# Fewer, larger transfers in a decode block: V's last two tiles in one, wo in 32 and 16 parts

## The chip, the cores and the metric

The kernel runs on one core of a Trainium2 chip. A core has TensorE (PE, matrix multiply), VectorE (DVE), ScalarE (ACT), GpSimd (POOL) and SyncE (SP), which here issues every DMA, and sixteen DMA engines that move the data from HBM (the chip's main memory) to SBUF (the core's working memory). Matmuls write to PSUM, in banks. The metric is the device time of one execution in microseconds (us), as the median of several runs; the profile describes one further execution.

## What is computed

One block of a transformer in decoding: two sequences of one token each, D = 640, 32 heads of 192, a window of the last 1024 positions of a cache of 4096, and a feed-forward part with F = 1536. All inputs are bfloat16.

```python
mod = (silu(c) @ w_mod).reshape(2, 6, 1, -1)
sa, ca, ga, sb, cb, gb = (mod[:, i] for i in range(6))
h = layernorm(x) * (1 + ca) + sa
q = (h @ wq).reshape(B, 1, 32, 192).transpose(0, 2, 1, 3)
k = k_cache[:, :, 3072:, :]; v = v_cache[:, :, 3072:, :]
p = softmax(einsum('bhqd,bhkd->bhqk', q, k) * 192 ** -0.5)
o = einsum('bhqk,bhkd->bhqd', p, v)
x = x + ga * (o.transpose(0, 2, 1, 3).reshape(B, 1, 6144) @ wo)
h = layernorm(x) * (1 + cb) + sb
x = x + gb * ((gelu(h @ w_gate) * (h @ w_up)) @ w_down)
```

K and V of the window are 25.2 MB each (32 heads, 1024 positions, 192 numbers of 2 bytes, two sequences), the largest share of the 76.88 MB that are read.

## The kernel before

**Memory.** `ring` has four slots of 24,576 bytes per partition, and `r1` takes the place of more: first it holds wq, then two tiles ("slots" 4 and 5), then wo. A tile of K or V is a quarter of one sequence's window: 128 partitions stand for 32 heads times four stretches of 256 positions, and a tile holds 64 of these positions for each. There are 16 tiles, eight of K and eight of V. The list `items` (line 336) says how they are loaded: kind, sequence, first tile, number of tiles, slot, semaphore. All entries take two tiles at once except the last two, which are tiles 2 and 3 of V of sequence 1, into slots 2 and 3. The semaphore counts 16 for each finished transfer (one for each DMA engine).

**The order of the transfers.** SyncE issues the transfers in the order of the program, and each issue waits for the instructions that last used the place that it overwrites. In order: w_mod, c, x, wq, the four K transfers, the V transfers, wo, w_gate, w_up, w_down in parts of 6, 4 and 2 of its twelve. `load_kv(n)` (line 344) issues `items` up to the n-th. The calls stand in the program where the place has just come free: the V transfers of sequence 1, tiles 2 and 3, come behind `weighted(0, 0, 2)`, because they overwrite tiles 0 and 1 of V of sequence 0 (slots 2 and 3). wo goes to `r1`, and its transfers wait for the last two PV steps of sequence 0 (line 603 on). w_gate, w_up and w_down go to slots 0 and 1 and wait for the first two PV steps of sequence 1 (`r3_dead`, line 607).

**The order of the work.** After the modulation, the first layer norm and q come the scores: DVE multiplies a half tile of K by q (line 465), PE sums with an identity matrix (line 476), DVE reduces (line 483). Then both softmaxes. Then PV: for each tile DVE spreads the weights over a mask (`d_mask`, line 511, two buffers in turn) and PE multiplies by the tile (`p_pv`, line 523, 32 matmuls of 384 columns). After the last tile of sequence 1 come `p_sel(0)` (line 548), `normalize(1)` (four small steps, ACT and DVE in turn, lines 536 and 540) and `p_sel(1)`. The result is copied out (lines 432 and 434) and turned by three DVE transposes of 16 parts each (line 597, `OT_SPLIT`).

**wo.** The 6144 rows of wo are 48 parts of 128 rows, a partition holding one row of each part. The parts are loaded and multiplied in groups, `WO_SPLIT`. A group's matmuls (line 628, four for each part, each on 32 columns of the array) wait for the group's transfer and for the transposes of its parts. The groups are multiplied in order.

**Fillers.** `warm(n, bank)` (line 454) puts n matmuls into PE's order whose result nobody reads; they keep PE busy. `WO_WARM` says how many follow each group of wo. Twelve follow the statistics of the second layer norm, eight follow w_gate, five w_up and five the first part of w_down.

**Behind wo.** Line 634 multiplies by ga, `layer_norm("ln2", ...)` ends with hT, w_gate's matmuls (line 646) feed the gelu on ACT (line 653), w_up's matmuls (line 646) the product on DVE (line 660) and its transpose, and w_down's three parts (line 669) follow. Two vector steps (lines 676 and 678) and the store of the output end the program.

Of the kernel before, what the change touches and what calls it, by code (L numbers as in the profile page):

```python
# [103 lines left out]
def bass_adaLN_cond__sliding_block_cached__geglu_ffn__decode_kernel(  # L104
# [49 lines left out]
    NS = 4  # L154
    SL = J * Dh
    WQ_SPLIT = [5]
    assert sum(WQ_SPLIT) == KT
    WO_SPLIT = [16, 16, 12, 4]
    OT_SPLIT = [16, 16, 16]
    assert sum(WO_SPLIT) == NT and sum(OT_SPLIT) == NT  # L160
    WU_SPLIT = [5]
# [2 lines left out]
    assert sum(WD_SPLIT) == FT  # L164
    ND = 4

    WO_WARM = [0, 8, 0, 9]
    WU_WARM = [5]
    WD_WARM = [5, 0, 0]

# [1 line left out]
    with es:  # L172
        S = _Sched(nc, es)
# [21 lines left out]
        def tile_f(slot, n=1):  # L195
            if slot < NS:
                return ring_f[:, slot * SL:(slot + n) * SL]
            return r1[:, (slot - NS) * SL:(slot - NS + n) * SL]
# [60 lines left out]
        def bank(k):  # L259
            return ("bank", k)  # L260
# [4 lines left out]
        sem_wq = [S.sem("d_wq%d" % i) for i in range(len(WQ_SPLIT))]  # L265
        sem_wo = [S.sem("d_wo%d" % i) for i in range(len(WO_SPLIT))]
        sem_wg = S.sem("d_wg")
        sem_wu = [S.sem("d_wu%d" % i) for i in range(len(WU_SPLIT))]
        sem_wd = [S.sem("d_wd%d" % i) for i in range(len(WD_SPLIT))]
        sem_ring = [S.sem("d_ring%d" % i) for i in range(4)]  # L270
        sem_out = S.sem("d_out")

        def k_dma(dst, src):
            return lambda e: e.dma_start(dst, src)  # L274
# [48 lines left out]
        def ring_keys(slot):  # L323
            return [half_key(slot, 0), half_key(slot, 1)]
# [9 lines left out]


        items = [("k", 0, 0, 2, 0, 0), ("k", 0, 2, 2, 2, 1), ("k", 1, 0, 2, NS, 2), ("k", 1, 2, 2, 0, 0), ("v", 0, 0, 2, 2, 1),
                 ("v", 0, 2, 2, NS, 2), ("v", 1, 0, 2, 0, 0), ("v", 1, 2, 1, 2, 1), ("v", 1, 3, 1, 3, 3)]
        place = {(kind, b, t0 + i): slot + i for kind, b, t0, nt, slot, _ in items for i in range(nt)}
        assert NTL == 4 and len(place) == 4 * NTL

# [3 lines left out]
        def load_kv(upto, deps=()):  # L344
            while keep["kv"] < upto:
                kind, b, t0, nt, slot, sm = items[keep["kv"]]
                cache = A_v_cache if kind == "v" else A_k_cache
                S.dma("sp", k_dma(tile_f(slot, nt),
                                  cache[b, :, K0:Sk, :].rearrange("h (q r) d -> h q r d", q=QP)[:, :, J * t0:J * (t0 + nt), :].rearrange("h q r d -> h q (r d)")),
                      sem_ring[sm], writes=[k for i in range(nt) for k in ring_keys(slot + i)], deps=deps, name="ld_%s%d_%d" % (kind, b, t0))  # L350
                keep["kv"] += 1
# [98 lines left out]
        def warm(n, bk):  # L450
            def f(e):
                last = None
                for _ in range(n):
                    last = e.matmul(ps[:, bk, 0:2 * Dh], lhsT=ident_b[:, :], rhs=qbc[:, :, :].rearrange("p b d -> p (b d)"),  # L454
                                    start=True, stop=True)
                return last
            if n:
                S.op("pe", f, reads=["ident_b", "qbc"], writes=[bank(bk)], name="warm")
# [104 lines left out]
        def weighted(b, ta, tb):  # L563
            for t in range(ta, tb):
                d_mask(b, t)
                p_pv(b, t)
# [10 lines left out]
        softmax(0)  # L577
        softmax(1)
        weighted(0, 0, 2)
        load_kv(9)  # L580
        weighted(0, 2, 4)
        normalize(0)
        for t in range(NTL):
# [17 lines left out]
        wo_src = A_wo.rearrange("(p t) n -> p t n", t=NT)  # L601
        wo_of = [(sum(WO_SPLIT[:i]), sum(WO_SPLIT[:i + 1])) for i in range(len(WO_SPLIT))]
        for i, (ta, tb) in enumerate(wo_of):
# [19 lines left out]
        for i, (ta, tb) in enumerate(wo_of):  # L623
# [7 lines left out]
            S.op("pe", f, reads=[("wo", i)] + [("oT", t) for t in range(ta, tb)], writes=[bank(BK_M)], name="wo%d" % i)  # L631
            warm(WO_WARM[i], 1)

# [82 lines left out]
```

## Time and profile before

| what | value |
|---|---|
| median of 3 runs | 187.02 us (186.99 to 187.12) |
| the profiled execution | 187.01 us |
| its span, first to last instruction | 185.7 us |
| PE, DVE, ACT, POOL busy | 117.2, 106.6, 13.9, 4.9 us |
| read from HBM | 76.88 MB, 414 GB/s over the span |
| mean granted clock of PE | 0.915 |

How to read what follows. Times count in microseconds from the first instruction. PEld is the loading of weights into PE, which overlaps the matmuls. The digits of a busy row are tenths in 40 equal slices of the span. A timeline's line gives the start, the length, the engine, the line of the program, the operation with its tiles and shapes, the count, and in brackets the idle time before it and what ended that. "DMA ring<-in_B_w_down_dram" is the stretch from a transfer's issue to its landing. A transfer is cut into packets, here one for each partition, and it has landed when all sixteen engines have written their last; beside the views, the trace records each packet's size and duration, the landing on each engine, and the times at which the granted clock changed. SPq is SyncE's queue of instructions.

### The profile page before, as it was taken

How to read it: one execution, taken by the hardware profiler on the slowest of the kernel's cores; microseconds unless marked ns; L12 is line 12 of the kernel's file. 1: busy time of each engine (PE TensorE's matmuls, PEld its weight loads, DVE VectorE, ACT ScalarE, POOL GpSimd, SP SyncE). 2: the span in 40 equal slices, each digit the busy share in tenths (PEclk: the TensorE clock that was granted, in tenths of full speed). 3: DMA queues.
4: the chain of work that ended last, by engine and by line, in shares of the span. 5: the costliest groups of instructions: out<-in, count | busy, mean ns of one | idle time of the engine just before them, and what ended most of it. 6: DMA issues, size and time to landing. Idle time of an engine off the chain costs nothing.

```text
span 185.7 us, 2254 instructions
## 1 busy us (share of the span) xinstructions
PE 117.2 (63%) x1014; PEld 60.8 (33%) x1014; DVE 106.6 (57%) x114; ACT 13.9 (7%) x24; POOL 4.9 (3%) x12
## 2 busy tenths in 40 slices
PE   0004500871079899988999885349928977299844
PEld 0001200440024334433344342226614654265422
DVE  6801600020598999999999993294556714803331
ACT  2001400013000000000000000200010004100400
POOL 8200000000000000000000000000000000000000
PEclk9999999998559999999999999558996999859999
DMA  7999998898999989899999989899999999999991
GB/s 248 414 437 477 463 463 389 371 491 371 487 413 434 468 381 459 381 487 402 455 424 434 459 381 466 381 487 413 395 434 424 424 435 424 413 408 435 422 392 50
DMA packets 2925, 77.02 MB, mean 415 GB/s; under 512 B 356, under 2 KB 356, under 8 KB 868
## 3 DMA queue, kind: packets, MB, share of 16 engines
q1 hardware_dynamic: 2916, 76.88, 96.7%
q8 instruction: 8, 0.13, 0.3%
q14 instruction: 1, 0.01, 0.0%
HBM read 76.88 MB, written 0.00 MB: 414 GB/s over the span
## 4 chain that ended last, share of the span: by engine, by line
DMA 43%; DVE 36%; PE 16%; SPq 1%; ACT 1%; issue 1%; POOL 1%; DVEq 0%; POOLq 0%
DMA ring<-in_A_k_cache_dram 24%; DVE ring L465 19%; DMA ring<-in_B_w_down_dram 18%; PE ps L523 10%; DVE r L465 7%; DVE Sg L483 5%; PE ps L476 4%; DVE Em L511 2%; SPq L274 1%; ACT E_sb L502 1%; PE ps L504 1%; PE ps L498 1%; DVE On L540 0%; ACT On L536 0%; PE ps L491 0%
## 5 line engine op out<-in xcount | busy, mean ns | idle before, releaser
L465 DVE TENSOR_TENSOR ring<-ring,qbc 128x6144 bf16<-128x6144 bf16 x12 | 40.1, 3351 | 8.4 <-DMA ring<-in_A_k_cache_dram 8.4
L476 PE MATMUL ps<-ring,ident_b 128*128 128x512 bf16 x144 | 34.7, 393 | 13.0 <-DVE ring L465 13.0
L454 PE MATMUL ps<-qbc,ident_b 128*128 128x384 bf16 x120 | 24.7, 339 | 0.7 <-ACT qbc L432 0.7
L523 PE MATMUL ps<-ring,Em 128*64 128x384 bf16 x192 | 19.6, 371 | 7.8 <-DVE Em L511 6.6
L476 PEld LDWEIGHTS ps<-ring,ident_b 128*128 128x128 bf16 x144 | 13.6, 100 | 32.7 <-DVE ring L465 17.2
L511 DVE TENSOR_TENSOR Em<-E_sb,M32b 128x2048 bf16<-128x2048 bf16 x8 | 18.1, 2288 | 5.5 <-PE ps L523 5.5
L523 PEld LDWEIGHTS ps<-ring,Em 128*64 128x64 bf16 x192 | 12.4, 125 | 14.6 <-DVE Em L511 7.3
L454 PEld LDWEIGHTS ps<-qbc,ident_b 128*128 128x128 bf16 x120 | 11.6, 101 | 10.9 <-issue 2.8
L401 PE MATMUL ps<-ring,scT 128*32 128x480 bf16 x40 | 4.4, 601 | 16.0 <-DVE scT L358 16.0
L465 DVE TENSOR_TENSOR r<-r,qbc 128x6144 bf16<-128x6144 bf16 x4 | 13.4, 3352 | 0.0
L483 DVE TENSOR_REDUCE Sg<-ps 128x32 f32<-128x512 f32 x16 | 11.0, 687 | 3.4 <-PE ps L476 3.4
L424 PE MATMUL ps<-r,hT 128*32 128x384 bf16 x80 | 5.8, 475 | 10.7 <-DMA r<-in_A_wq_dram 10.7
L476 PE MATMUL ps<-r,ident_b 128*128 128x512 bf16 x48 | 11.1, 380 | 1.8 <-DVE r L465 1.8
L434 DVE CAST aux<-ps 128x384 bf16<-128x384 f32 x4 | 2.0, 553 | 16.6 <-PE ps L424 15.7
L628 PE MATMUL ps<-r,aux 128*32 128x160 bf16 x192 | 5.1, 271 | 4.4 <-DMA r<-in_A_wo_dram 2.6
L424 PEld LDWEIGHTS ps<-r,hT 128*32 128x32 bf16 x80 | 3.2, 135 | 13.8 <-issue 11.6
L476 PEld LDWEIGHTS ps<-r,ident_b 128*128 128x128 bf16 x48 | 4.4, 98 | 8.1 <-DVE r L465 3.4
L401 PEld LDWEIGHTS ps<-ring,scT 128*32 128x32 bf16 x40 | 1.2, 132 | 17.5 <-DVE scT L358 16.0
L540 DVE TENSOR_SCALAR On<-ps,rden 32x192 bf16<-32x192 f32 x4 | 1.7, 418 | 8.9 <-ACT On L536 8.9
L502 ACT ACTIVATE E_sb<-Sg,nb 128x256 bf16<-128x256 f32 x2 | 1.0, 507 | 75.6 <-DVE nb L501 75.6
L628 PEld LDWEIGHTS ps<-r,aux 128*32 128x32 bf16 x192 | 4.3, 114 | 5.8 <-DMA r<-in_A_wo_dram 3.6
L523 PE MATMUL ps<-r,Em 128*64 128x384 bf16 x64 | 5.4, 327 | 0.0
(73 smaller groups left out, 65.6 us busy)
## 6 DMA issues: line engine op xcount, KB each, us to landing
ring<-in_A_k_cache_dram SPq DMA_DIRECT2D x3, 6144.0 KB, 40.3
ring<-in_A_v_cache_dram SPq DMA_DIRECT2D x2, 6144.0 KB, 23.3
r<-in_A_wq_dram SPq DMA_DIRECT2D x1, 7680.0 KB, 30.7
r<-in_A_k_cache_dram SPq DMA_DIRECT2D x1, 6144.0 KB, 38.4
r<-in_A_v_cache_dram SPq DMA_DIRECT2D x1, 6144.0 KB, 23.3
ring<-in_A_v_cache_dram SPq DMA_DIRECT2D x2, 3072.0 KB, 17.6
r<-in_A_wo_dram SPq DMA_DIRECT2D x2, 2560.0 KB, 23.7
ring<-in_w_mod_dram SPq DMA_DIRECT2D x1, 4800.0 KB, 14.2
```

Source lines behind the costliest of these rows:

```text
L274: return lambda e: e.dma_start(dst, src)
L401: last = e.matmul(ps[SQ * j:SQ * j + SQ, bk, 0:3 * DN].rearrange("p (i n) -> p i n", i=3), lhsT=scT[:, k, :], rhs=wm_v[:, k, 3 * part * D: ...
L424: last = e.matmul(ps[SQ * j:SQ * j + SQ, BK_H + c, 0:QC], lhsT=hT[:, k, :], rhs=wq_v[:, k, RN * j + QC * c:RN * j + QC * (c + 1)], start=( ...
L434: S.op("dve", lambda e: e.tensor_copy(out=dst, in_=src), reads=reads, writes=writes, name=name)
L454: last = e.matmul(ps[:, bk, 0:2 * Dh], lhsT=ident_b[:, :], rhs=qbc[:, :, :].rearrange("p b d -> p (b d)"), start=True, stop=True)
L465: S.op("dve", lambda e: e.tensor_tensor(out=tile_v(ks)[:, hf * JH:(hf + 1) * JH, :], in0=tile_v(ks)[:, hf * JH:(hf + 1) * JH, :], in1=qbc[ ...
L476: last = e.matmul(o_ap, lhsT=ident_b[:, :], rhs=tile_v(ks)[:, hf * JH:(hf + 1) * JH, ci * GC:(ci + 1) * GC], start=(ci == 0), stop=(ci == ...
L483: S.op("dve", lambda e: e.tensor_reduce(out=S_sb[:, b, a:a + JH], in_=ps[:, hf, 0:JH * GC].rearrange("p (j c) -> p j c", j=JH), axis=AX.X, ...
L502: S.op("act", lambda e: e.activation(out=E_sb[:, b, :], in_=S_sb[:, b, :], func=ACTF.Exp, scale=SCALE, bias=nb[:, 0:1], accum_out=esum[:, ...
L511: S.op("dve", lambda e: e.tensor_tensor(out=Em[:, t % 2, :, :], in0=E_sb[:, b, J * t:J * (t + 1)].unsqueeze(2).broadcast_to([P, J, H]), in ...
L523: last = e.matmul(ps[r:r + 2 * H, BK_O, 0:ON], lhsT=Em[:, t % 2, 2 * jp:2 * jp + 2, :].rearrange("p j c -> p (j c)"), rhs=tile_v(vs)[:, 2 ...
L628: last = e.matmul(ps[SQ * j:SQ * j + SQ, BK_M, 0:DN], lhsT=oT[:, t, :], rhs=wo_v[:, t, DN * j:DN * j + DN], start=(t == 0), stop=(t == NT ...
```

## The change

Three transfers fewer. Tiles 2 and 3 of V of sequence 1 are loaded by one transfer of 6144 KB into slots 2 and 3, with the semaphore that the first of them used; it waits for the last use of both slots. The call that issued the two entries now issues the one (`load_kv(8)`). wo comes in two groups, of 32 and 16 parts, in place of four of 16, 16, 12 and 4; the fillers behind the groups are 8 and 9, where they were 0, 8, 0 and 9. The transposes stay in three groups of 16.

```diff
-    WO_SPLIT = [16, 16, 12, 4]
+    WO_SPLIT = [32, 16]
     OT_SPLIT = [16, 16, 16]
...
-    WO_WARM = [0, 8, 0, 9]
+    WO_WARM = [8, 9]
...
-        sem_ring = [S.sem("d_ring%d" % i) for i in range(4)]
+        sem_ring = [S.sem("d_ring%d" % i) for i in range(3)]
...
-                 ("v", 0, 2, 2, NS, 2), ("v", 1, 0, 2, 0, 0), ("v", 1, 2, 1, 2, 1), ("v", 1, 3, 1, 3, 3)]
+                 ("v", 0, 2, 2, NS, 2), ("v", 1, 0, 2, 0, 0), ("v", 1, 2, 2, 2, 1)]
...
         weighted(0, 0, 2)
-        load_kv(9)
+        load_kv(8)
         weighted(0, 2, 4)
```

## The prediction

> **What bounds the kernel now.** I read the busy rows first: no engine passes 63%, but the sixteen DMA engines are occupied from the first microseconds to the last.
>
> ```profile
> DMA  7999998898999989899999989899999999999991
> q1 hardware_dynamic: 2916, 76.88, 96.7%
> ```
>
> The chain that ended last says the same of the end. Its last pieces (start, length, what):
>
> ```profile
> 148.89 33.92 DMA ring<-in_B_w_down_dram
> 182.81 0.04 issue
> 182.85 0.35 PE ps L669 x8
> 183.20 0.02 issue
> 183.22 0.34 DVE lnt L676
> ```
>
> The third part of w_down is issued at 148.89 and lands 33.92 us later: it stood in a queue. Only 8 matmuls, two vector operations and the store of the output come behind it. So the end is when the byte stream ends, as long as TensorE (PE) is ready by then. The timeline shows what PE does while the stream runs out (start, length, engine, line, what, count, and in brackets the idle time before and what ended it):
>
> ```profile
> 123.50 7.05 PE L523 MATMUL ps<-ring,Em 128*64 128x384 bf16 x64 [2.45 <-DVE Em L511]
> 128.04 3.09 SPq L274 DMA_DIRECT2D ring<-in_A_v_cache_dram  x2
> 130.41 5.39 PE L523 MATMUL ps<-r,Em 128*64 128x384 bf16 x64
> ...
> 150.84 2.79 PE L523 MATMUL ps<-ring,Em 128*64 128x384 bf16 x32 [1.14 <-DMA ring<-in_A_v_cache_dram]
> 157.49 4.12 DVE L597 STREAM_TRANSPOSE aux<-aux 128x512 bf16<-128x512 bf16 x3
> 159.08 1.29 PE L628 MATMUL ps<-r,aux 128*32 128x160 bf16 x64 [1.79 <-DVE aux L597]
> 162.78 2.33 PE L628 MATMUL ps<-r,aux 128*32 128x160 bf16 x64 [2.41 <-DMA r<-in_A_wo_dram]
> ...
> 169.00 0.46 PE L628 MATMUL ps<-r,aux 128*32 128x160 bf16 x16 [0.21 <-DMA r<-in_A_wo_dram]
> 174.09 1.00 PE L646 MATMUL ps<-ring,hT 128*32 128x384 bf16 x20 [0.61 <-DVE hT L358]
> 178.18 1.00 PE L646 MATMUL ps<-ring,hT 128*32 128x384 bf16 x20 [1.69 <-DMA ring<-in_B_w_up_dram]
> 182.25 0.93 PE L669 MATMUL ps<-ring,aux 128*32 128x160 bf16 x24
> ```
>
> Every stage with a DMA in its brackets waits for the stream; w_up's matmuls at 178.18 are the last large one. Two granted clocks show in the same work: 64 PV matmuls take 5.39 us, but 7.05 us where the first 3.4 us ran at the half clock; 64 wo matmuls take 1.29 or 2.33 us. The windows view gives the clock:
>
> ```profile
> 147.39:150.81 3.42, 2.32 (x30) 1.36 (x24) 2.07 (x1) 0.00 (x0) 0.00 (x0) 1.00 1.00 423
> 161.05:164.46 3.41, 1.68 (x52) 1.68 (x56) 0.56 (x1) 0.00 (x0) 0.00 (x0) 0.50 1.02 427
> 164.46:167.88 3.42, 3.42 (x36) 1.53 (x32) 0.00 (x0) 0.00 (x0) 0.00 (x0) 0.50 1.00 419
> ```
>
> (Stretch, length, busy us of PE, weight loads, DVE, ACT, POOL; then clock, DMA share, GB/s.) All clock records change on a grid of 3.41 us. A stretch with PE busy for 0.58 us (137.16 to 140.57) was followed by one at 0.50, one with 1.68 busy stayed at 0.50 in the next, one with 1.79 (174.70 to 178.11) was followed by 1.00, and a fully busy one always was.
>
> **The change, part by part.** The sum is made against the profiled execution, 187.01 us (span 185.7, 1.3 around it); the median shown, 187.02, is the same.
>
> *DMA stream.* Packet by packet, the trace has a median of 915 ns for 24,576 bytes and 1816 ns for 49,152, so a row of V in one packet saves some 14 ns; each engine carries 8 rows: about 0.07 us by the undisturbed packets (912 against 1815). For wo a row takes 2×761 + 573 + 196 = 2291 ns now. 40,960 bytes, between the measured 38,400 (1420 ns) and 49,152 (1815 ns), come to 1514 ns; with 761 for the second that is 2275. 16 ns × 8 rows = 0.13 us. Three completion writes of 9 ns fall away: 0.03. Sum: 0.23 us off the stream; I use 0.22. For the size of the unknown: the two single V tiles landed (last engine) 7.30 and 7.50 us after what stood before them, where half of a pair (14.53 us) is 7.27. So a transfer's price lies between nothing and 0.23 us, three of them between 0 and 0.7. I take 0.22, because packets of just these sizes are in the trace, and keep both ends.
>
> *SyncE.* Three issues of 0.43 to 0.54 us fall away, hidden under a queue of some 15 us. The joined V transfer must now wait for PV of both tiles that it overwrites, so it is issued at about 130.6, where its second half was, not at 128.04. The engines' first packet of it is needed at 133.6, when the first engine has done its part of the pair before. An issue into an empty queue took 1.0 us (w_mod, 0.80 to 1.80) to 1.35 us (the output, 183.93 to 185.28) to the first packet: 131.9. The cover is 1.7 us; what exceeded it would be paid in full at the end. Queued behind the waiting issue on SyncE are wo's, which wait until 135.84 for the fourth PV anyway.
>
> *PV of the last two tiles.* Now the third tile's matmuls run at 146.92 beside the wait for the fourth. Joined, both tiles land when the fourth did, and 64 matmuls begin at 150.75 in place of 32. PE is idle from 147.1 until then, so the stretch 147.39 to 150.81 is empty and the next has the half clock. The nearest row is the first PV pair, which met the same: 7.05 us. End 157.80, not 153.63: 4.17 later. The lower bound is the row at full clock, 5.39 (2.5 later).
>
> *Selection and transposes.* One chain without slack: all 4.17 later. The three transposes of 1.37 us then end at 163.0, 164.4 and 165.8.
>
> *wo, first 32 parts.* They land where parts 16 to 31 did (162.74, less 0.14). But the second transpose, at 164.4, comes later: this stage's wait passes from DMA to DVE. PE is idle from 161.5 to 164.4, so this too begins at half clock: 35 ns a matmul (2.26 us for 64) against 17 (1.06 for 63). Of 128 matmuls 97 pass by 167.88, and 31 more end at 168.4. Then the 8 fillers, at 0.163 each: 169.7.
>
> *wo, last 16 parts.* They land with the end of wo, 168.95 less 0.22, before PE is free. 64 matmuls, 1.29 us: 171.0. Before it was 169.46, so this stage comes 1.54 late. The wait that ends last here is PE itself.
>
> *To w_up.* Line 634 to hT takes 4.52 us, unchanged: w_gate's matmuls begin at 175.63. From their start to the end of the 8 fillers now takes 2.40 us (174.09 to 176.49): PE is free at 178.03. w_up lands at 178.14 less 0.22 and could start at 177.96. The wait of 1.69 us on w_up is used up by the lateness, with 0.07 us over.
>
> *The end.* From w_up's start the work needs 4.69 us of its own: the second w_down part landed at 182.02 (landing records) and began at 182.25, behind fillers; its 16 matmuls (0.27) and the last 8 (0.35) would end at 182.87; actually 183.20, because of the landing. That is 0.33 us of slack. w_up starts 0.15 earlier than before, the last landing is 0.22 earlier, so the landing still ends last. Sum: −0.22 us at the end, **186.8**.
>
> **A rule against the change.** The Trainium skill, *TensorE: Matmul & The Clock Gate*, Part 1, says that the clock's window is free-running and not tied to the kernel's start. The grid of 3.41 us agrees with the page's 3413 ns; that its phase moves between executions no run here shows. By that rule, the two half-clock stretches could lie otherwise against the work: PE's readiness for w_up would scatter by something under a microsecond, and the sum above would become anything from 186.8 to about 187.2.
>
> **The rivals.**
> *PE becomes the bound (slower).* Mechanism: the half clock at the first wo part isn't lifted after one stretch, because matmuls of 32 columns in a stretch of mere wo work count too little. For it: no stretch filled by wo alone has been followed by 1.00 (the one at 164.46 held 8 fillers). Against: PE was busy for all of it, and the first clock record, at 38.17, grants the full clock after q's equally narrow matmuls had run alone since 33.34. Price at most: 128 × 35.3 ns = 4.5, 8 fillers at the half-clock row's 2.74 us, 1.29: wo would end at 173.0, w_up start at 180.0, 1.8 late, less 0.33 of slack: +1.5, 188.5. It decides from a w_up start of 178.51 on (slower than before); from 178.9 on the loss is over 0.2%.
> *A transfer costs more than its packets (faster).* With 0.23 us each, 186.3. Against it: wo's part of 640 KB lands 1.57 us after the one before it, and its 8 packets of 196 ns are 1.57.
> The Trainium skill, *DMA: Bandwidth & Descriptors*, section on the anatomy of one DMA, gives a fixed cost of about 2.0 us per DMA, mostly the wait for the write's receipt (measured there on GpSimd's path); paid per transfer it would make 181.0. That spacing of 1.57 us speaks against it: whatever is fixed overlaps with the next transfer.
> *The queue runs dry at 133.6 (slower).* It needs 3.0 us from issue to first packet; the most seen is 1.35. Even with the slowest issue on record, 2.35 us, it comes to 133.6: price about 0.
>
> **How the numbers follow.** About 0.2% (0.37 us) is what a measurement of this kernel can tell from no change. The forecast of 186.8: 0.63. PE the bound by a little, within 0.2%: 0.07. PE the bound by more: 0.18. A higher price per transfer: 0.11 (that of 2 us each: under 0.01). A dry queue: 0.01. So faster 0.11, same 0.70, slower 0.19. The range goes from 186.5, half-way to the high transfer price, to 187.7, about half-way to PE's highest price; some 0.07 lie outside on either side.
>
> **What would show it.** Right: 64 PV matmuls at about 150.8 taking some 7 us; wo in two groups, the first released by the transposes; no DMA in front of the last wo group; w_up's start near 178.0 with a tiny wait; the last w_down landing at 182.6. Wrong: a w_up start beyond 178.5, a clock of 0.50 after 167.9, or a DMA share that dips at 133.

## The result, and the profile after

| | before | after |
|---|---|---|
| median | 187.12 us (186.88 to 187.26, 22 runs) | 187.41 us (186.87 to 190.0, 22 runs) |
| ratio | | 1.0032, 95% interval 1.0016 to 1.0047 |
| profiled execution | 187.01 us | 187.24 us |

The change makes the kernel slower by 0.3%, and it makes it uneven: the executions before lie within 0.4 us, those after within 3.1. (An execution more than 1.5% above the fastest of its kernel is left out of the ratios here.) The same kernel run again in three more groups gave ratios of 1.0047 (1.0025 to 1.007), 1.0018 (1.0006 to 1.0029) and 1.0055 (1.0032 to 1.0079). The medians of these three groups were 187.94, 187.40 and 188.12 us. The forecast was 186.8 us, with 0.70 on no change that can be told.

The page of the changed kernel shows as full a set of DMA engines as before, with 432 packets fewer:

```profile
DMA  7999998898999989899998989899989899999991
q1 hardware_dynamic: 2484, 76.88, 96.6%
```

The end of its chain (start, length, what) is of the old kind, a landing with 8 matmuls and a little vector work behind it. But the landing is at 183.12, not at 182.6 as forecast, and 0.31 us later than before:

```profile
151.49 31.63 DMA ring<-in_B_w_down_dram
183.12 0.04 issue
183.16 0.35 PE ps L669 x8
183.51 0.02 issue
183.53 0.34 DVE lnt L676
```

The timeline's lines for the steps of the forecast:

```profile
124.30 8.04 PE L523 MATMUL ps<-ring,Em 128*64 128x384 bf16 x64 [2.45 <-DVE Em L511]
132.43 0.54 SPq L274 DMA_DIRECT2D ring<-in_A_v_cache_dram  x1
151.11 5.39 PE L523 MATMUL ps<-ring,Em 128*64 128x384 bf16 x64 [1.49 <-DMA ring<-in_A_v_cache_dram]
163.29 3.97 PE L628 MATMUL ps<-r,aux 128*32 128x160 bf16 x128 [3.12 <-DVE aux L597]
169.46 1.29 PE L628 MATMUL ps<-r,aux 128*32 128x160 bf16 x64 [0.77 <-DMA r<-in_A_wo_dram]
178.50 1.00 PE L646 MATMUL ps<-ring,hT 128*32 128x384 bf16 x20 [0.71 <-DMA ring<-in_B_w_up_dram]
```

PE is in time: it waits 0.77 us for the last of wo and 0.71 us for w_up. What is late is the second line. The joined V transfer is issued at 132.43; the forecast had 130.6. The windows view (stretch, length, busy time of PE, weight loads, DVE, ACT and POOL, then clock, DMA share and GB/s) gives a first sign of what that does. Before:

```profile
132.00:134.00 2.00, 2.00 (x28) 1.30 (x26) 0.96 (x1) 0.00 (x0) 0.00 (x0) 1.00 0.89 377
134.00:136.00 2.00, 1.81 (x24) 1.03 (x18) 0.00 (x0) 0.15 (x1) 0.00 (x0) 1.00 0.85 356
```

After:

```profile
132.00:134.00 2.00, 2.00 (x30) 1.35 (x26) 1.58 (x2) 0.00 (x0) 0.00 (x0) 1.00 1.13 426
134.00:136.00 2.00, 2.00 (x28) 1.27 (x26) 0.75 (x1) 0.00 (x0) 0.00 (x0) 1.00 0.65 246
```

The 246 GB/s between 134 and 136 us stand against 356 before. They are a sign and no measure: the view counts a packet whole in the stretch in which it begins (hence shares above 1.00), and over 130 to 138 us the two executions come to 401 and 404 GB/s. The packet records are clearer. Twelve packets of the joined transfer begin between 133.76 and 135.50 and take 2.02 to 2.67 us where 1.82 is usual; most end together, at 136.26 to 136.49. Less 1.82, the data of these ten began to flow at about 134.5, 2.0 to 2.2 us behind the issue; this reading is worked out from the ends, the records have no time for it. The first engine had been free at 133.64. The queue had run dry. On the mean over the engines the joined transfer landed at 149.74, against 149.52 for the later of the two single tiles before.

Why the issue is later can be read from the clock. It waits for the first two PV steps, and these come later by 0.80 us (124.30 for 123.50) and take 0.99 us longer (8.04 for 7.05). The first part can be followed back to the first sum of the scores. Before and after:

```profile
52.03 4.33 PE L476 MATMUL ps<-ring,ident_b 128*128 128x512 bf16 x12 [8.71 <-DVE ring L465]
```

```profile
52.19 5.30 PE L476 MATMUL ps<-ring,ident_b 128*128 128x512 bf16 x12 [9.25 <-DVE ring L465]
```

Neither is touched by the change. The clock's grid lay elsewhere: the full clock was granted at 55.23 in the one execution, at 58.05 in the other, and in front of PV at 126.92 and 129.73. Over the profiles of this study the first clock record lies between 35.6 and 39.2 us, spread over a whole step of 3.41 us: the grid's phase is not tied to the kernel. In the two profiles of the kernel before, the first single-tile transfer is issued one PV earlier, at 128.04 and 128.43, and the queue holds.

### The profile page after: what moved, and what is told of

It is laid out like the page before. It is cut to its first block, busy times and chain, and to the rows that moved or that the text cites. A ratio compares the mean times of both kernels' runs of the same rounds, so it can differ in the third digit from the quotient of the medians.

```text
span 186.0 us, 2249 instructions
## 1 busy us (share of the span) xinstructions
PE 118.5 (64%) x1014; PEld 62.3 (34%) x1014; DVE 106.6 (57%) x114; ACT 13.9 (7%) x24; POOL 4.9 (3%) x12
## 4 chain that ended last, share of the span: by engine, by line
DMA 42%; DVE 36%; PE 17%; SPq 1%; ACT 1%; issue 1%; POOL 1%; DVEq 0%; POOLq 0%
DMA ring<-in_A_k_cache_dram 25%; DVE ring L465 19%; DMA ring<-in_B_w_down_dram 17%; PE ps L523 11%; DVE r L465 7%; DVE Sg L483 5%; PE ps L476 4%; DVE Em L511 2%; SPq L274 1%; ACT E_sb L502 1%; PE ps L504 1%; PE ps L498 1%; DVE On L540 0%; ACT On L536 0%; DVE M L489 0%
## 5 line engine op out<-in xcount | busy, mean ns | idle before, releaser
L476 PE MATMUL ps<-ring,ident_b 128*128 128x512 bf16 x144 | 35.7, 401 | 13.3 <-DVE ring L465 13.3
L523 PE MATMUL ps<-ring,Em 128*64 128x384 bf16 x192 | 21.3, 394 | 8.1 <-DVE Em L511 6.6
L454 PE MATMUL ps<-qbc,ident_b 128*128 128x384 bf16 x120 | 23.9, 330 | 0.7 <-ACT qbc L432 0.7
L523 PEld LDWEIGHTS ps<-ring,Em 128*64 128x64 bf16 x192 | 13.7, 133 | 15.4 <-DVE Em L511 7.1
L628 PEld LDWEIGHTS ps<-r,aux 128*32 128x32 bf16 x192 | 4.8, 121 | 4.6 <-DMA r<-in_A_wo_dram 4.6
```

What stands on the lines that cost most here:

```text
L476: last = e.matmul(o_ap, lhsT=ident_b[:, :], rhs=tile_v(ks)[:, hf * JH:(hf + 1) * JH, ci * GC:(ci + 1) * GC], start=(ci == 0), stop=(ci == ...
L523: last = e.matmul(ps[r:r + 2 * H, BK_O, 0:ON], lhsT=Em[:, t % 2, 2 * jp:2 * jp + 2, :].rearrange("p j c -> p (j c)"), rhs=tile_v(vs)[:, 2 ...
L628: last = e.matmul(ps[SQ * j:SQ * j + SQ, BK_M, 0:DN], lhsT=oT[:, t, :], rhs=wo_v[:, t, DN * j:DN * j + DN], start=(t == 0), stop=(t == NT ...
```

## The experiments

Two accounts stood against each other. *Dry queue:* the joined transfer waits for the second PV of sequence 0, whose end moves with the clock's grid, and from 133.6 us on engines stand idle. *PE late:* both last tiles, and wo in two groups, come later to PE, which then holds up the end. (Where fillers are added, the numbers of the lines behind them shift by up to 7: PV, line 523, becomes 528 in most.)

**One half of the change alone: V joined.** wo stays in 16, 16, 12 and 4 parts.

```diff
-    WO_SPLIT = [32, 16]
+    WO_SPLIT = [16, 16, 12, 4]
...
-    WO_WARM = [8, 9]
+    WO_WARM = [0, 8, 0, 9]
```

> V's last two tiles in one transfer as in the change, wo in its four groups as before. Dry queue (the joined transfer is issued only when the second PV of sequence 0 has ended, the time of that moves with the clock's grid between executions, data flow some 2.0 us behind the issue, and what is past 133.6 us is lost at the end of the stream): the loss and the scatter of the changed kernel stay, median 187.2 to 187.6, single executions up to 188 and over, and in the profile the first engine's landing of the joined transfer lies 14.5 us plus the gap behind the one before it. PE late because wo comes in two groups behind the transposes: with four groups the median falls to 187.0 or below and the scatter to that of before (0.4 us).

Measured: 187.47 us (186.97 to 188.93, 12 runs), ratio 1.0036 (1.0016 to 1.0057). Loss and scatter are all here.

**The other half: wo in 32 and 16, V's tiles in two transfers.**

```diff
-    WO_SPLIT = [16, 16, 12, 4]
+    WO_SPLIT = [32, 16]
...
-    WO_WARM = [0, 8, 0, 9]
+    WO_WARM = [8, 9]
```

> wo in 32 and 16 parts as in the change, V's last two tiles in two transfers as before. Dry queue: nothing is left of the loss; the stream is 0.15 us shorter, median 186.9 to 187.0, scatter as before. PE late through wo's grouping: median 187.3 to 187.6 with single executions over 188, and w_up's matmuls no longer wait for their landing.

Measured: 186.99 us (186.85 to 187.40, 11 runs), ratio 0.9996 (0.9987 to 1.0004). Not to be told from before. So wo's grouping does no harm that can be told by itself.

**Only the time of the issue.** The kernel before, with its two single-tile transfers; the first waits as the second does.

```diff
-        load_kv(9)
+        load_kv(9, deps=[keep["pv", 0, 1]])
```

> The kernel before with one difference: the first of the two single-tile V transfers waits, as the second does, for the second PV of sequence 0. Two transfers, four wo groups, the third tile still lands alone and early. Dry queue: the lateness of the issue does it, not the joining, so median 187.2 to 187.6 with the scatter of the changed kernel. PE late: the third tile's PV runs before the fourth lands, so PE is as early as before, median 187.1, scatter 0.4 us.

Measured: 188.20 us (187.22 to 188.77, 6 runs), ratio 1.0053 (1.0032 to 1.0074). Nothing is joined, and the third tile's PV runs as early as ever; the loss is there. So the delay of the issue is enough for a loss of this size; the joined transfer has such a delay by its nature.

**The time of the issue given back.** The same kernel with 25 fillers in the gaps of the two softmaxes (4 + 1 + 3 + 2 in and before the first, 2 + 3 + 10 in the second; the expectations count them as 29), so that PV begins nearer to the full clock.

```diff
-        load_kv(9)
+        load_kv(9, deps=[keep["pv", 0, 1]])
...
         def softmax(b):
+            if b == 0:
+                warm(4, BK_W)
...
              reads=["M1", "ident_f"], writes=[bank(BK_T)], name="T%d" % b)
+            warm(1 + b, BK_W)
...
              writes=[bank(BK_T)], name="Bc%d" % b)
+            warm(3, BK_W)
...
              writes=[bank(BK_T)], name="den%d" % b)
+            warm((2, 10)[b], BK_W)
```

> The kernel with two single-tile transfers of which the first is issued as late as the second, plus the 29 fillers in the softmaxes. Dry queue: the issue comes near 129.5 us, and the loss of 0.5% that this kernel had without the fillers goes: median 187.0 to 187.15, scatter 0.4 us. If the loss had another cause than the time of the issue, 187.7 to 188.2 stays.

Measured: 187.04 us (186.88 to 187.71, 12 runs), ratio 0.9998 (0.9988 to 1.0008). SyncE's lines, without and with the fillers:

```profile
130.50 1.18 SPq L274 DMA_DIRECT2D ring<-in_A_v_cache_dram  x2
```

```profile
129.16 1.18 SPq L274 DMA_DIRECT2D ring<-in_A_v_cache_dram  x2
```

Some 1.3 us earlier, and the 0.5% are gone. The fillers act on PE too, but its end in this profile is as before (1.13 us from the last landing to the store's issue, table below). The first of the two lines is from the best execution of its kernel, 187.22 us; one of 188.13 us, below, had the issue at 131.16.

**A larger dose.** The changed kernel with the joined transfer waiting for the third PV.

```diff
         weighted(0, 0, 2)
-        load_kv(8)
-        weighted(0, 2, 4)
+        weighted(0, 2, 3)
+        load_kv(8, deps=[keep["pv", 0, 2]])
+        weighted(0, 3, 4)
```

> The changed kernel with the joined transfer waiting for the third PV of sequence 0 instead of the second, 2.6 us more. Dry queue: the stream stops for these 2.6 us more, engine by engine, and the last w_down part lands 2 to 3 us later than with the change (183.1), near 185.5 us: 189.5 to 190.5. If the queue had cover left at the changed kernel's issue, less than 2 us.

Measured: 188.94 us (188.83 and 189.05), ratio 1.0095 (1.0076 to 1.0115), the last landing at 184.71. The issue came at 134.00, 1.57 us later than in the profile of the changed kernel, not 2.6 us, because here the earlier PV lay well in the grid. On the mean over the sixteen engines the last landing came 1.27 us later (183.41 for 182.14): 0.8 us for each. Both numbers stay below those expected, which had assumed an issue 2.6 us later. In the windows the packets that should begin before 134 us are missing:

```profile
132.00:134.00 2.00, 2.00 (x28) 1.32 (x26) 1.68 (x1) 0.00 (x0) 0.00 (x0) 1.00 0.63 270
134.00:136.00 2.00, 2.00 (x28) 1.40 (x26) 0.00 (x0) 0.00 (x0) 0.00 (x0) 1.00 1.33 426
```

The first engine was free at 133.61; fifteen packets recorded from 135.32 on took 2.4 to 2.65 us: by the same subtraction, the flow began 2.0 to 2.3 us behind the issue, as in the changed kernel.

**The changed kernel with the 25 fillers.**

> The changed kernel with 29 more fillers on PE in the gaps of the two softmaxes (4 before them, then 1 to 10 behind each of their matmuls), so that PV begins at the full clock. Dry queue: the first two PV take about 5.4 us instead of 7 to 8, the joined transfer is issued near 129.5 us, the gap in the stream is gone, median 186.8 to 186.95, scatter as before. PE late: the joined tiles land as late as ever and nothing behind them changes, so median 187.3 to 187.5 and executions over 188 as in the changed kernel.

Measured: 187.71 us (186.74 to 188.97, 12 runs), ratio 1.0034 (1.0014 to 1.0054). This speaks for the other account: the issue came at 129.46, no first packet of the joined transfer is stretched, the last landing is at 182.76, and the time is no better. The end of the chain of this execution (188.28 us) has no DMA in it behind the joined V:

```profile
150.83 8.33 PE ps L528 x64
...
165.93 3.47 PE ps L633 x128
169.40 1.95 PE ps L454 x8
...
178.53 1.41 PE ps L454 x8
179.94 0.96 PE ps L651 x20
```

PV of the two tiles took 8.33 us and w_up starts at 179.9 behind fillers, 1.8 us after its landing at 178.11. The windows show the half clock under the first 6 us of it:

```profile
149.99:153.40 3.41, 2.57 (x18) 1.72 (x20) 0.00 (x0) 0.00 (x0) 0.00 (x0) 0.50 0.97 420
153.40:156.81 3.41, 3.41 (x24) 2.27 (x22) 0.00 (x0) 0.00 (x0) 0.00 (x0) 0.50 0.92 396
```

PE was busy for 2.57 us of the first stretch, 75%, and the second still had the half clock. So each account is true of some execution, the second so far only with fillers in the program.

**The fillers behind the second PV of sequence 1 alone**, to keep the clock up to the joined landing: 14 there, 18 for 6 behind the last selection, 18 for 8 behind wo's first part.

```diff
-    WO_WARM = [8, 9]
+    WO_WARM = [18, 9]
...
             p_pv(1, t)
+            if t == 1:
+                warm(14, 1)
...
-        warm(6, 1)
+        warm(18, 1)
```

> The changed kernel with the fillers behind the second PV of sequence 1 alone (14 there, 18 behind the last selection, 18 behind the first wo part), none in the softmaxes. If a dry queue is the larger of the two costs: median 187.2 to 187.4 still, executions up to 188; the end is set by the landing of w_down in the profile. If PE late is the larger one: 186.9 to 187.0, executions no higher than 187.5.

Measured: 187.26 us (186.80 to 189.61, 12 runs), ratio 1.0017 (0.9997 to 1.0037). The median is the one expected if the dry queue costs more; five executions lie above the 188 expected. The profiled execution, 188.39 us, has a dry queue (issue 131.83, seventeen stretched packets) and PE waiting 1.57 us for w_up. Its stream is later than that of the changed kernel's first profile (mean landing 182.56 against 182.14), though its issue is 0.6 us earlier: the time of the issue alone does not give the size of the loss.

**Both sets of fillers**, with 26 for the 14.

> The changed kernel with both suspected costs taken away by fillers alone: the 29 in the softmaxes (the joined transfer is issued early) and, new, 26 between the second and third PV of sequence 1, 18 in place of 6 behind the last selection and 18 in place of 8 behind the first wo part (PE keeps the full clock and is ready for every landing). Both costs, a dry queue in front of the joined transfer and PE late behind it: 186.75 to 186.9, scatter 0.4 us or less. If something else in the joined transfers costs time, 187.2 or more stays.

Measured: 12 executions in two heaps, 186.78 to 187.19 and 191.62 to 194.37; the ratio over the lower heap is 0.9986 (0.9975 to 0.9997). The lower heap is what the theories asked for. The upper one nobody expected, it has no profile, and its cause stays open.

**Both sets, fewer** (14 and 10, 8 as before behind wo's first part).

> The changed kernel with the 29 fillers in the softmaxes, 14 fillers between the second and third PV of sequence 1 and 10 in place of 6 behind the last selection: both costs taken away with fillers that end well before the landings. 186.8 to 187.0, no execution over 187.6. If the 14 fillers are too few to hold the full clock up to the landing, the executions of 188 and more stay.

Measured: 188.53 us (186.75 to 190.02, 12 runs), ratio 1.0068 (1.0042 to 1.0093). Two executions of 186.8, all others over 188: the expected 186.8 to 187.0 did not come, and the only profile is that of the execution of 186.75 us. What the others lost stays open.

**The 25 fillers, and the 8 between the wo parts taken out.**

```diff
-    WO_WARM = [8, 9]
+    WO_WARM = [0, 9]
```

> The changed kernel with the 29 fillers in the softmaxes (the queue does not run dry) and without the 8 fillers between the two wo parts (PE has 1.3 to 2.0 us less to do between the joined landing and w_up). PE late: what was left of the loss with the 29 fillers alone (executions of 187.3 to 189.0) shrinks by 1.3 to 2 us, so nearly all executions lie between 186.75 and 187.2, median 186.85 to 187.0. If what is left has another cause, median 187.3 to 187.7 and the scatter stay.

Measured: 187.15 us (186.63 to 188.41, 12 runs), ratio 1.0017 (1.0001 to 1.0033). The median is lower than with the 8, though the intervals overlap, and not as low as expected. In the profile PE stops in the middle of wo's last part (the chain):

```profile
168.74 0.53 PE ps L633 x19
169.27 1.44 issue
170.71 1.02 PE ps L633 x45
```

"issue": it waits for nothing that the profile shows. At 168.21 the instruction queue (q8) fetched 16 KB, which took 0.99 us.

**V joined, wo in four, with the 25 fillers.**

> V joined, wo in its four groups, with the 29 fillers in the softmaxes. PE late through the joined V alone: the scatter of the changed kernel with these fillers stays (median 187.2 to 187.8, executions over 188.3), since the fourth and third tile's matmuls stand behind one landing all the same. PE late only together with wo's two groups: median 187.0, scatter 0.5 us.

Measured: 187.17 us (186.83 to 188.94, 11 runs), ratio 1.0014 (0.9996 to 1.0033). Between the two expectations; it decides nothing. In its profile PE stops for 2.26 us in the same way, with a fetch at 167.8.

**More profiles: the changed kernel three times, the kernel before and the late split transfers once more.**

> The changed kernel itself once more, for a second profile: a joined issue between 130.5 and 133 us, and behind it either a gap in the stream of up to 1 us, or PE late at w_up, or both. If neither shows where the execution is over 187.4 us, the account of the loss is wrong.

> The changed kernel once more, for a further profile. The last landing lies at 183 us or later and the mean over the engines over 181.9 where the joined issue comes later than about 131.5 (dry queue); a single engine over 1.5 us behind the mean shows as in the execution of 189.6; or PE ends more than 2.9 us after the last landing.

> As the look before it: the excess over 186.8 us is the sum of a late mean landing, of the slowest engine's lag behind the mean beyond 0.9 us, and of PE's work behind the last landing beyond that of the kernel before; nothing else is left over by more than 0.2 us.

> The kernel before, for a second profile: the slowest engine lags the mean of the last landing by 0.9 us again (0.87 in the first profile), within 0.3, since its queue is never dry; if it too shows a lag of 1.5 us or more, the lag has nothing to do with the change.

> Two single-tile transfers, the first issued as late as the second, for a profile of one of its slower executions: above 187.7 us, with a late mean landing or a single engine's lag behind 133.6 us, and PE waiting for w_up as before (1.69 us).

Medians: 187.94, 187.40 and 188.12 us for the changed kernel, 187.18 for the one before (ratio 1.0001, 0.999 to 1.0012), 188.15 for the late split (1.005, 1.0021 to 1.0078). The use is in the profiled executions. From the landing records (us): the issue that had to fill the queue, the mean over the sixteen engines of the last w_down landing, the slowest engine's lag behind that mean, and the time from that landing to the issue of the store.

| execution | time | issue | mean landing | lag | to the store |
|---|---|---|---|---|---|
| before | 187.01 | 128.04 | 181.94 | 0.86 | 1.13 |
| before, again | 187.23 | 128.43 | 181.95 | 1.16 | 1.13 |
| changed | 187.24 | 132.43 | 182.14 | 0.98 | 1.13 |
| changed, again | 189.60 | 131.95 | 182.06 | 3.32 | 1.13 |
| changed, third | 187.76 | 132.15 | 182.06 | 1.58 | 1.13 |
| changed, fourth | 187.19 | 132.19 | 182.04 | 0.94 | 1.13 |
| wo alone | 186.99 | 127.74 | 181.75 | 1.04 | 1.13 |
| V joined alone | 187.28 | 131.30 | 182.06 | 1.10 | 1.13 |
| late split | 187.22 | 130.50 | 181.95 | 1.05 | 1.13 |
| late split, again | 188.13 | 131.16 | 182.22 | 1.30 | 1.62 |
| late split, 25 fillers | 187.14 | 129.16 | 181.92 | 1.10 | 1.13 |
| larger dose | 188.83 | 134.00 | 183.41 | 1.30 | 1.13 |
| 25 fillers | 188.28 | 129.46 | 181.62 | 1.14 | 2.54 |
| 14, 18 and 18 fillers | 188.39 | 131.83 | 182.56 | 1.71 | 1.13 |
| 25 fillers, 8 taken out | 187.07 | 129.58 | 181.66 | 0.88 | 1.55 |

The last three columns add up, by the way they are made, to the time of the store's issue; they show where the lateness lies and not why. Against the first row, 189.60 is +0.12 on the mean and +2.46 on the lag (189.59); 187.76 is +0.12 and +0.72 (187.85); 188.28 is −0.32, +0.28 and +1.41 (188.38); no more than 0.1 is left over. In all four executions of the changed kernel PE cost nothing; the stream was 0.10 to 0.20 us late on the mean, and up to 2.5 us later on one engine. In the late split of 188.13 us, 0.28 is the mean, 0.44 the lag, and 0.49 PE, whose clock fell at 178.98 after 1.96 us of waiting for w_up. The second profile of the kernel before lags by 1.16 us, within the 0.3 us expected around 0.87.

The lag is the part that is only half explained. In the execution of 189.60 us, one engine in sixteen (a share of 0.06) works on alone from 182.6 on, by the packet records; the last window has a fetch of instructions beside it. The windows:

```profile
182.00:183.00 1.00, 0.72 (x5) 0.20 (x3) 0.96 (x2) 0.00 (x0) 0.00 (x0) 1.00 0.13 54
183.00:184.00 1.00, 0.59 (x25) 0.46 (x26) 0.36 (x1) 0.00 (x0) 0.00 (x0) 1.00 0.07 31
184.00:185.00 1.00, 1.00 (x17) 0.49 (x17) 0.00 (x0) 0.00 (x0) 0.00 (x0) 1.00 0.11 37
```

The lag was 2.16 us when the joined V landed, against 0.99 to 1.24 in the other three, and grew from 2.02 to 3.60 between the two wo landings, where a fetch of instructions (at 169.68, 1.01 us) held an engine. The first part can be followed in the packet records, in which an engine is known by each packet beginning where the one before it ends: one engine was free at 134.07, began its first packet of the joined transfer at 135.87 only and took 2.90 us for it. It is the one that ends the joined transfer last, at 151.52. So the greater part of this lag came from the dry queue itself. A fetch holds one engine for about 1 us (0.88 to 1.42 in all kernels here), and the packet behind it is stretched by about 0.5. Where the issue came by 131.4 us, the lag was 0.86 to 1.31 (12 profiles); where it came later, 0.94 to 3.32 (6 profiles). That a dry queue sets the engines apart, so that a fetch can hit one that is behind already, fits all this, but beyond the one execution it is not shown: which engine a fetch goes to could not be chosen, and an earlier fetch without a dry queue was not tried.

## Why the prediction was wrong

The range, 186.5 to 187.7, held the first median, 187.41, but not 187.94 and 188.12, two of the three later ones; the forecast itself, 186.8 with no difference that can be told, was on the wrong side. That the first median lies inside is luck: the upper part of the range stood for PE becoming the bound, and none of the four profiles of the changed kernel shows that. Point by point:

*The gain of the stream, 0.23 us: right.* Where the queue did not run dry, the mean landing moved from 181.94 to between 181.62 and 181.76 (0.18 to 0.32, the four profiles with both joinings and an issue by 129.8), and with wo alone to 181.75 (0.19, for a forecast 0.15). The smaller count of packets is worth what the packets' durations say. The higher price of 0.23 us per transfer, the faster rival, is out, as is the 2.0 us.

*SyncE, "the cover is 1.7 us": this is the step that failed, twice.* First, 130.6 was taken from one execution for the time at which the second PV ends. In the four profiles of the changed kernel it was 131.95 to 132.43. Second, 1.0 to 1.35 us from issue to first packet was read from the starts of packets. A packet that finds the queue empty is recorded as begun long before its data flow: 2.0 to 2.3 us passed on most engines. (The output's 1.35 us runs to its last packet; its first is recorded at 185.20, 1.27 us behind the issue.) w_mod's first packets, there to be read before, had shown it (the longest took 2.88 us where 1.42 is the median). So 133.6 was missed by about 0.8 us instead of being met with 1.7 to spare. Nor would the forecast's own issue time have been safe: with the issue at 130.50 (late split), one packet begun at 133.60 took 1.71 us where 0.91 is usual. The rival *The queue runs dry*, at a price of about 0 and a chance of 0.01, is what happened. Its mechanism and its place were right. The sum also had no term for the slowest engine's lag behind the mean: it left the 0.86 us of its one profile as they were, and in the changed kernel they were 0.94 to 3.32.

*The clock: two stretches that can't be compared.* The forecast put side by side a stretch with 1.68 us busy that stayed at 0.50 and one with 1.79 that was followed by 1.00. The second had the full clock already. No threshold on PE's busy time comes out of the profiles. Of 3.41 us, 2.45 (changed kernel, 51.23) and 2.57 (25 fillers, 149.99) did not lift the clock, and 2.82 did (wo alone, 51.43); but 3.36 did not (25 fillers, 8 taken out, 117.06). And 1.79 kept the full clock, where 2.45 did not (late split with fillers, 116.92). What the forecast needed was the phase: in the changed kernel's profile the first PV pair ran at the half clock from 124.30 to 129.73, 5.4 us, against 3.4 before (123.50 to 126.92). That is why it took 8.04 us, which moved the issue.

*The rule against the change.* The Trainium skill (TensorE: Matmul & The Clock Gate, Part 1) says that the clock's window runs free of the kernel, and the profiles agree, with remainders all over 3.41 us. The forecast weighed it at the wrong place: it scattered PE's readiness for w_up, and left the issue of the transfer, which waits for PE too, at a fixed time.

*PV of the joined tiles: 7.05 us was one of its two values.* 5.39 in three of the four profiles of the changed kernel, 7.07 in the other; both ends stood in the forecast.

*wo and w_up.* The first part was released by a transpose, as forecast, and took 3.97 us (forecast: 164.4 to 168.4); in the third and fourth profile it was the landing of wo that released it. PE was free for w_up at about 177.8 (forecast 178.03) and waited 0.71 us, because the landing had moved to 178.46.

*PE becomes the bound.* Not seen in the four profiles of the changed kernel. Seen with the 25 fillers, where the queue did not run dry: 8.33 us of PV, 1.41 us at the end. Its place and size are those of the rival (up to 1.5 us), it comes from the joined tiles' PV at the half clock and not, as the rival had it, from wo's narrow matmuls alone (3.47 us there for the first 32 parts, 3.97 in the changed kernel). How often it costs the unaltered change something stays open: four profiles can't say.

## What to carry to other kernels

A transfer that is joined with its neighbour is issued when the later of their two places is free. Before it is called hidden, the time of that issue must be taken at its latest, over the phases of the clock, and not from the one execution that the profile shows. And the lead that a full queue needs is to be read from the ends of the first packets behind an empty queue: here some 2 us on most engines and 4 to 5 us on single ones, where their starts suggest 1.0 to 1.35.

## What was not expected of the hardware

How long PE is busy in a 3.41 us stretch does not tell the next granted clock: 3.36 us once did not lift it and 2.82 us did, 1.79 us once kept it and 2.45 us did not.

A packet's recorded duration includes the wait for its first data when the queue has been empty: 2.02 to 2.67 us for 49,152 bytes that take 1.82 otherwise. Single engines waited longer than the rest: by the same subtraction their data began 3.9 us behind the issue with V joined alone (two packets, 3.20 and 3.40 us) and in one execution of the late split, 4.2 in the other, and 5.0 in the changed kernel's execution of 189.60 us, while packets begun beside them took the usual time. Why single engines wait so long stays open.

Instructions are fetched 16 KB at a time, and the packet records show a transfer's next packet beginning where a fetch ends (134.67 in the changed kernel). PE may stand still for a fetch: 1.44 us within one run of wo matmuls with the fetch at 168.2, 2.26 us with a fetch at 167.8. That the fetch is what PE waited for is read from the times alone, and in the changed kernel no such stop stands beside the fetch at 167.35.

Fillers meant to hold the clock made two heaps of executions, some 5 us apart. No profile shows the upper one.
